# The second MLP product of six token chunks in seven block products for eight, with the sums on GpSimd and all of it in 128x64 tiles

## The chip, the cores and the metric

The kernel runs on one core of a Trainium2 chip. The metric is the device time of one execution in microseconds (us); lower is better. Five engines matter: PE (TensorE, the matrix unit, with its weight loads shown as PEld), DVE (VectorE), ACT (ScalarE), POOL (GpSimd), and SP, whose queue issues most of the DMAs.

## The reference, cut to what matters

The input of the MLP is the output of a linear attention with 4 batches, 4 heads, 1088 tokens and head width 32. The tokens are the rows of a 4352 x 128 matrix. The MLP goes to 2048 hidden channels and back to 128.

```python
def phi(x):                       # 64 features of a token: all products of two 8-wide sketches
    a = np.einsum('rd,bhsd->bhsr', S1, x)
    b = np.einsum('rd,bhsd->bhsr', S2, x)
    return np.einsum('bhsi,bhsj->bhsij', a, b).reshape(*x.shape[:-1], r * r)
q_p, k_p = (phi(q), phi(k))
kv = np.einsum('bhsf,bhsd->bhfd', k_p, v)
z = np.sum(k_p, axis=2)
x = (q_p @ kv) / (q_p @ z + 1e-06)          # per batch and head
...
x = np.ascontiguousarray(attn_out.transpose(0, 2, 1, 3)).reshape(B * S, H * D)   # 4352 x 128
h = x @ w_in                                 # 4352 x 2048
g = 0.5 * h * (1.0 + erf(h * inv_sqrt2))
return (g @ w_out).astype(np.float32)        # 4352 x 128
```

The change is about the last line, `g @ w_out`.

## The kernel before, in words

**Chunks and steps.** The tokens are cut into nine chunks: chunks 0 to 7 have 512 tokens each (two a batch, `NMAIN = 8`), chunk 8 has the 64 last tokens of each batch, 256 in all. The 2048 hidden channels are cut into 16 tiles of 128 (`NF`). One step is one chunk `n` and one tile `fi`. The list `steps` has 144 of them: chunks 0 and 1 alternate in groups of four, and from step 32 on it is chunk after chunk, 16 steps each.

**What a step does.** `hidden(n, fi)` multiplies a 128x128 tile of `w_in` with the turned attention output `xT[n]` (128 channels x 512 tokens) into a PSUM bank (`h_ps`, two buffers, line 488), and ACT takes it through Gelu into a tile `g` (line 490). `project`, two steps later (`LAG = 2`), multiplies a 128x128 tile of `w_out` with that `g` and adds it up over the 16 tiles in one PSUM bank (`o_ps`, two buffers, line 503). All values are fp32, and a product of fp32 values is two matmul instructions. When the 16 tiles are done, `store` turns the bank with one DVE transpose (line 513) and issues the DMAs to the output.

**The attention of later chunks** is put into steps of earlier ones by the calls `at(t, f, ...)`: `slots[t]` holds what is issued in step `t`. For chunk `n` that is `query_turn` (a DVE transpose), `query_expand` (four matmuls at line 393, four ACT copies at line 400 into the tile `A_sb`, four DVE multiplications at line 414) and `attend` (matmuls at line 434, four ACT copies into `den` at line 440, a DVE reciprocal at line 441, four DVE multiplications at line 445 that write `xT[n]`). For batch `b` it is `widen_v` and `widen_v_rem` on POOL (lines 287 and 295, with memsets), `key_turn_blocks` (four DVE transposes, line 304), `features` (matmuls at line 319, copies on ACT, multiplications on DVE at line 333), `finish_keys` (matmuls at lines 353 and 360) and `turn_kv` (a transpose on PE, line 369). They use the four PSUM banks of `w_ps`.

**The weights** come in as 64-bit numbers and are rounded to fp32 in the kernel by `Rounding`, piece by piece (`CUTS`), during chunks 0 and 1.

**Order.** Each engine takes its instructions in the order of the text; a loop at the end of the function adds dependencies that keep it. Within a step the order is `hidden`, then `store` of a finished chunk, then `slots[t]`, then `project_at(t)`:

```python
    def project_at(t):
        if LAG <= t < len(steps) + LAG:
            project(*steps[t - LAG])
            if steps[t - LAG][1] == NF - 1:
                done.append(steps[t - LAG][0])
```

Of the kernel before, what the change touches and what calls it, by code (L numbers as in the profile page):

```python
# [8 lines left out]
FP = mybir.dt.float32  # L9
U32 = mybir.dt.uint32  # L10
# [6 lines left out]
def kernel(  # L17
# [18 lines left out]
    pe, dve, act, pool, sp = nc.tensor, nc.vector, nc.scalar, nc.gpsimd, nc.sync  # L36
# [3 lines left out]
    d_model = out.shape[1]  # L40
    d_ff = moe_w_in.shape[1]
    NF = d_ff // 128
# [5 lines left out]
    CW = JC * 128  # L48
    G = 128 // 32
    NCH = J // JC  # L50
    C = D + 1
    LAG = 2
    NMAIN = B * NCH
    NCHUNK = NMAIN + 1
    assert B == 4 and d_model == 128 == H * D == JC * D == 2 * F and H == 4 and REM == 64 and NCH == 2

    big = ctx.enter_context(tc.tile_pool(name="big", bufs=1))
    att = ctx.enter_context(tc.tile_pool(name="att", bufs=2))
    mlp = ctx.enter_context(tc.tile_pool(name="mlp", bufs=2))
# [8 lines left out]
    def work_bank():  # L68
        return work_banks()[:, 0]
# [7 lines left out]
    def out_bank():  # L77
        return ops.tile([128, CW], FP, name="o_ps")
# [4 lines left out]
    LC = 512  # L83
    pieces = list(zip(CUTS, CUTS[1:]))
# [30 lines left out]
    def load_rem(n, b):  # L115
        sp.dma_start(out=rem[n][b // 2 * REM:(b // 2 + 1) * REM, b % 2],
                     in_=src_of[n][b, :, MAIN:S, :].rearrange("h p d -> p h d"))

    def landing(dst, wide):

        if wide:
            raw[dst.name] = big.tile([dst.shape[0], dst.shape[1], 2], U32, name=f"raw_{dst.name}")
            return raw[dst.name].rearrange("p n two -> p (n two)")
        return dst

# [247 lines left out]
    qT, qp, xT = {}, {}, {}  # L373
# [104 lines left out]
    g_of, o_of = {}, {}  # L478

    def w_tile(w, fi):  # L480
        i = max(i for i, (c0, c1) in enumerate(pieces) if c0 <= fi * 128)
        at = fi * 128 - CUTS[i]
        return w[i][:, at:at + 128]

    def hidden(n, fi):
        W = width[n]
        ps = hidden_bank()
        pe.matmul(ps[:, :W], lhsT=w_tile(w_in_sb, fi), rhs=xT[n][:, :W], start=True, stop=True)  # L488
        g_of[n, fi] = mlp.tile([128, CW], FP, name="g", bufs=4)
        act.activation(out=g_of[n, fi][:, :W], in_=ps[:, :W], func=ACT.Gelu)  # L490

    def project(n, fi):
        first, final = fi == 0, fi == NF - 1
        if first:
            o_of[n] = out_bank()
        g = g_of.pop((n, fi))
        if n == NMAIN:

            for i in range(B // 2):
                pe.matmul(o_of[n][:, i * 128:(i + 1) * 128], lhsT=g[:, i * 128:(i + 1) * 128], rhs=w_tile(w_out_sb, fi),  # L500
                          start=(first and i == 0), stop=final, skip_group_check=True)
            return
        pe.matmul(o_of[n], lhsT=w_tile(w_out_sb, fi), rhs=g, start=first, stop=final)  # L503
    def store(n):
        oT = mlp.tile([128, JC, d_model], FP, name="oT")
        if n == NMAIN:
            for i, (copy, eng) in enumerate(((by_dve, sp), (by_act, act))):
                copy(out=oT[:, i, :], in_=o_of[n][:, i * 128:(i + 1) * 128])  # L508
                for b in (i, i + 2):
                    eng.dma_start(out=out[b * S + MAIN:(b + 1) * S, :], in_=oT[b // 2 * REM:(b // 2 + 1) * REM, i, :])  # L510
            return

        dve.transpose(out=oT.rearrange("p n d -> p (n d)"), in_=o_of[n])  # L513
        row = n // NCH * S + n % NCH * CW
        if n < NCH:
# [17 lines left out]
    bank = work_bank()  # L533
    keep_busy(3, bank)
    r = Rounding(SR)
# [72 lines left out]
    def at(t, f, *a):  # L608
        slots[t].append(lambda: f(*a))
# [29 lines left out]
    for i, (t0, t1) in enumerate(((4, 6), (8, 10), (12, 20))):  # L639
        round_at(t0, w_in_sb[i + 2])  # L640
        round_at(t1, w_out_sb[i + 2])
    for b in range(1, B):
        t = NCH * b * NF
        for r in range(2):
            at(t - 20, widen_v, b, r)
        at(t - 20, widen_v_rem, b)
        for r in range(2):
            at(t - 18, key_turn_blocks, b, r)
        for r in range(2):
            at(t - 17, features, b, r)  # L650
        if b == 1:
            at(t - 16, turn_keys_rem, b)
            at(t - 15, features_rem, b)
        at(t - 14, finish_keys, b)
        at(t - 13, lambda b=b: turn_kv(b, held["kv"], by_dve))
    for n in range(2, NCHUNK):
        t = n * NF
        at(t - 13, query_turn, n)
        at(t - 12, query_expand, n)
        at(t - 8, attend, n)  # L660

    def project_at(t):
        if LAG <= t < len(steps) + LAG:
            project(*steps[t - LAG])
            if steps[t - LAG][1] == NF - 1:
                done.append(steps[t - LAG][0])

    done = []
    for t in range(len(steps) + LAG):
        if t == 3:  # L670

            attend_by_token(1, halves(work_banks()), lambda: (w_out[1].mantissas(), w_out[1].signs(),
                                                              w_out[1].product(pool)))
        if t == 4:
            turn_x(1, work_bank())
            project_at(t)
        if t < len(steps):
            hidden(*steps[t])
        while done:
            store(done.pop())  # L680
        for f in slots[t]:
            f()
        if t != 4:
            project_at(t)
    while done:
        store(done.pop())


    last = {}
# [36 lines left out]
```

## Time and profile before

| what | before |
|---|---|
| median of 3 runs | 289.57 us (288.95 to 289.64) |
| the profiled execution, its own time | 289.47 us |
| its span in the profile | 287.3 us |
| granted TensorE clock | 0.998 |
| busy PE, DVE, ACT, POOL | 280.7, 121.8, 134.4, 15.6 us |
| matmul instructions of `hidden` (line 488) | 288 |
| matmul instructions of `project` (line 503 / chunk 8, line 500) | 256 / 64 |

The span is the time from the first to the last instruction in the profile; the 2.2 us between it and the execution's time lie around it. A row of a group gives line, engine and operation, output and inputs, shapes and count, then busy time, the mean of one in ns, and the idle time of the engine just before these instructions with what ended it. A row of the timeline gives start, duration, engine, line, and how many instructions are merged in it. Matmuls overlap in the pipeline, so what counts for PE is the distance from start to start and not the duration of one.

### The profile page before, as it was taken

The numbers are of one execution on the slowest core, as the hardware profiler recorded it, in microseconds if no ns is written. First come the engines' busy times: TensorE is split into PE (matmuls) and PEld (weight loads), VectorE is DVE, ScalarE is ACT, GpSimd is POOL, SyncE is SP. The second block draws the span as 40 slices with busy tenths as digits, with TensorE's granted clock in tenths as the row PEclk, the third lists the DMA queues.
The fourth block names the chain that finished last, engine by engine and source line by source line (L and its number), as shares of the span: only waits on it lengthen the run. The fifth ranks groups of instructions, "written<-read, shape, count | busy, mean of one in ns | idle before, by whom it ended". The sixth has DMA issues, their size and how long they took to land.

```text
span 287.3 us, 3822 instructions
## 1 busy us (share of the span) xinstructions
PE 280.7 (98%) x1479; PEld 135.8 (47%) x1479; DVE 121.8 (42%) x196; ACT 134.4 (47%) x258; POOL 15.6 (5%) x44
## 2 busy tenths in 40 slices
PE   8989999999999999999999999999999999999994
PEld 6744444643444344543444344544444344444793
DVE  5996888163713093233513184234313351231000
ACT  4683774266335633255335533256335633453341
POOL 3331040300000000300000000000000000000000
PEclk9999999999999999999999999999999999999999
DMA  7568532535012000200001000200010000100010
GB/s 210 174 196 277 140 82 65 167 73 147 2 30 34 9 0 2 37 2 0 0 12 27 0 2 0 39 0 0 0 28 10 0 0 9 27 2 0 16 20 18
DMA packets 37904, 13.36 MB, mean 46 GB/s; under 512 B 28288, under 2 KB 37248, under 8 KB 37888
## 3 DMA queue, kind: packets, MB, share of 16 engines
q1 hardware_dynamic: 37648, 13.05, 18.2%
q8 instruction: 11, 0.18, 0.3%
q10 hardware_dynamic: 240, 0.08, 0.1%
q14 instruction: 5, 0.04, 0.0%
HBM read 10.90 MB, written 2.23 MB: 46 GB/s over the span
## 4 chain that ended last, share of the span: by engine, by line
PE 96%; DVE 1%; ACT 0%; issue 0%
PE h_ps L488 41%; PE o_ps L503 39%; PE w_ps L393 3%; PE o_ps L500 2%; PE w_ps L434 2%; PE w_ps L353 2%; PE w_ps L531 1%; PE w_ps L319 1%; PE o_ps L353 1%; PE h_ps L274 1%; PE h_ps L459 0%; PE w_ps L459 0%; PE o_ps L274 0%; DVE xT L473 0%; DVE bits_a L224 0%
## 5 line engine op out<-in xcount | busy, mean ns | idle before, releaser
L490 ACT ACTIVATE g<-h_ps 128x512 f32<-128x512 f32 (+1 forms) x144 | 82.5, 573 | 127.7 <-PE h_ps L488 127.4
L488 PE MATMUL h_ps<-xT,w_in 128*128 128x512 f32 (+1 forms) x288 | 140.2, 570 | 1.1 <-DVE xT L473 1.0
L503 PE MATMUL o_ps<-g,w_out 128*128 128x512 f32 x256 | 132.9, 601 | 0.0
L488 PEld LDWEIGHTS h_ps<-xT,w_in 128*128 128x128 f32 x288 | 53.4, 190 | 63.8 <-issue 60.0
L503 PEld LDWEIGHTS o_ps<-g,w_out 128*128 128x128 f32 x256 | 46.5, 190 | 59.0 <-issue 57.7
L441 DVE RECIPROCAL den<-den 128x512 f32<-128x512 f32 (+1 forms) x7 | 21.9, 3124 | 44.0 <-ACT den L440 44.0
L414 DVE TENSOR_TENSOR q_pT<-A_sb,w_ps 64x512 f32<-64x512 f32 x32 | 22.1, 691 | 24.0 <-ACT A_sb L400 23.3
L513 DVE STREAM_TRANSPOSE oT<-o_ps 128x512 f32<-128x512 f32 x8 | 5.7, 717 | 43.9 <-PE o_ps L503 43.9
L400 ACT COPY A_sb<-w_ps 64x512 f32<-64x512 f32 (+1 forms) x36 | 17.7, 557 | 3.1 <-PE w_ps L393 3.0
L445 DVE TENSOR_TENSOR xT<-w_ps,den 32x512 f32<-32x512 f32 (+1 forms) x28 | 18.2, 649 | 1.0
L440 ACT ACTIVATE den<-w_ps 32x512 f32<-32x512 f32 (+1 forms) x28 | 15.6, 557 | 3.0 <-PE w_ps L434 2.7
L333 DVE TENSOR_TENSOR k_p<-a_t,w_ps 128x512 f32<-128x512 f32 x12 | 8.0, 686 | 7.9 <-ACT a_t L332 7.9
L287 POOL COPY v_aug<-v 128x512 f32<-128x512 f32 x8 | 5.5, 699 | 86.3 <-PE w_ps L353 73.2
L500 PEld LDWEIGHTS o_ps<-w_out,g 128*128 128x128 f32 x64 | 9.3, 191 | 0.7
L500 PE MATMUL o_ps<-w_out,g 128*128 128x128 f32 x64 | 9.4, 274 | 0.0
L393 PE MATMUL w_ps<-qT,Srep 32*128 32x512 f32 x64 | 9.1, 640 | 0.0
L230 ACT ACTIVATE bits_r<-bits_e,below 128x512 uint32<-128x512 uint32 (+2 forms) x11 | 6.7, 611 | 1.5 <-DVE bits_e L222 1.4
L434 PE MATMUL w_ps<-q_pT,kz 64*64 64x512 f32 (+1 forms) x80 | 7.2, 458 | 0.0
L353 PEld LDWEIGHTS w_ps<-k_p,v_aug 128*64 128x64 f32 x192 | 5.8, 138 | 2.3 <-issue 2.3
L238 DVE SCALAR_TENSOR_TENSOR bits_m<-bits_a,bits_low 128x512 f32<-128x512 uint32 (+2 forms) x10 | 5.8, 584 | 2.4 <-ACT bits_low L218 1.7
L353 PE MATMUL w_ps<-k_p,v_aug 128*64 128x64 f32 x192 | 6.3, 224 | 0.0
L508 DVE COPY oT<-o_ps 128x128 f32<-128x128 f32 x1 | 0.3, 291 | 12.5 <-PE o_ps L500 12.5
(119 smaller groups left out, 114.6 us busy)
## 6 DMA issues: line engine op xcount, KB each, us to landing
raw_w_in<-in_moe_w_in_dram SPq DMA_DIRECT2D x3, 512.0 KB, 6.6
raw_w_out<-in_moe_w_out_dram SPq DMA_DIRECT2D x3, 512.0 KB, 9.5
k<-in_k_dram SPq DMA_DIRECT2D x48, 32.0 KB, 1.8
v<-in_v_dram SPq DMA_DIRECT2D x3, 512.0 KB, 4.3
q<-in_q_dram SPq DMA_DIRECT2D x24, 64.0 KB, 3.7
out_dram<-oT SPq DMA_DIRECT2D x24, 64.0 KB, 2.2
k<-in_k_dram SPq DMA_DIRECT2D x2, 256.0 KB, 2.9
q<-in_q_dram SPq DMA_DIRECT2D x2, 256.0 KB, 3.8
```

Source lines behind the costliest of these rows:

```text
L353: pe.matmul(ps[c * 64:(c + 1) * 64, r * F:(r + 1) * F], lhsT=v_aug[:, 2 * c + r, i, :], rhs=k_p[b, r][:, t, c * 4 + ch * 2 + one].rearrang ...
L393: pe.matmul(B_of[n][g // 2][:, g % 2, :W], lhsT=Srep[rows].rearrange("p a i j -> p (a i j)"), rhs=qT[n][rows].rearrange("p h j t -> p (h j ...
L400: act.copy(out=A[g // 2][F:, g % 2, :width[n]], in_=B_of[n][g // 2][:F, g % 2, :width[n]])
L414: dve.tensor_mul(out=cols[r * F:(r + 1) * F], in0=a[:, :, r::2], in1=b[:, :, r::2])
L434: pe.matmul(banks[r][c * F:(c + 1) * F, c0:c1], lhsT=kz[b][r * F:(r + 1) * F, c, :], rhs=qp[n][r * F:(r + 1) * F, c, c0:c1], start=True, s ...
L440: act.activation(out=den[h * D:(h + 1) * D, :W], in_=banks[r][at:at + D, :W], func=ACT.Copy, bias=1e-6)
L441: dve.reciprocal(out=den[:, :W], in_=den[:, :W])
L445: dve.tensor_mul(out=xT[n][rows, :W], in0=banks[h % 2][rows, :W], in1=den[rows, :W])
L488: pe.matmul(ps[:, :W], lhsT=w_tile(w_in_sb, fi), rhs=xT[n][:, :W], start=True, stop=True)
L490: act.activation(out=g_of[n, fi][:, :W], in_=ps[:, :W], func=ACT.Gelu)
L500: pe.matmul(o_of[n][:, i * 128:(i + 1) * 128], lhsT=g[:, i * 128:(i + 1) * 128], rhs=w_tile(w_out_sb, fi), start=(first and i == 0), stop= ...
L503: pe.matmul(o_of[n], lhsT=w_tile(w_out_sb, fi), rhs=g, start=first, stop=final)
```

## The change

**The product by blocks.** For chunks 2 to 7 the second product is computed in blocks: the 512 tokens in two halves of 256, the 128 output channels in two halves of 64, and the tiles `fi` in pairs. For one pair, that is a 2x2 by 2x2 product of blocks, eight block products of 128x64 weights by 256 tokens in the plain form. The new form makes seven of them from sums of blocks, numbered 1 to 7 (6 is added in two places, `6a` and `6b`). `channel_sums` makes the sums of weight blocks (`T[1]` to `T[4]`), once for each piece of `w_out`. `token_sums` makes four sums of blocks of `g`, for four steps (`NB = 4`, two pairs) at a time. Both are on POOL.

**Tiles.** Two block products are issued together, one into partitions 0 to 63 and one into 64 to 127 of PSUM, so each uses one half of the array's columns (`PLACE` has half, bank and column). A chunk adds up in both `o_ps` banks. `hidden` of these chunks, and of the first five tiles of chunk 8, is issued as two products of 64 columns each instead of one of 128.

**Putting the parts together.** `combine(n)` copies both banks to SBUF (one by DVE, one by ACT), moves parts between the halves of the partitions with two more ACT copies, and makes six additions on DVE. `store` turns its result.

**Order.** The block products of four steps are issued as 3, 2 and 2 pairs, 3 to 5 steps after the last of the four (first block of a chunk), or as 2, 2, 1 and 2 pairs, 2 to 5 steps after it (other blocks). `store` and `combine` of a chunk come in step 5 of the next chunk, ahead of `slots[t]`. The keys of batches 2 and 3 and the turning and expanding of queries from chunk 3 on come two steps earlier; `attend` stays. The products of chunk 8's first tiles are put later, behind the last block products of chunk 7.

**Buffers.** The landing buffers of the raw weights become tiles of two rings (`block`, three buffers, and `small`, four), which later hold `g` and the weight sums. The token sums take over the tiles of `Rounding`, and `combine` those of `A_sb`. The DMAs and their order stay as they were.

```diff
--- before.py
+++ after.py
@@ -51,6 +51,8 @@
     C = D + 1
     LAG = 2
     NMAIN = B * NCH
+    FAST = 2
+    NB = 4
     NCHUNK = NMAIN + 1
...
+    def block(dtype=U32):
...
+        b = big.tile([128, NB, 512], U32, name="block", bufs=3)
...
+    def small(dtype):
...
+        t = big.tile([128, 512], U32, name="small", bufs=4)
...
-    def hidden(n, fi):
+    def hidden(n, fi, by_halves=False):
         W = width[n]
         ps = hidden_bank()
-        pe.matmul(ps[:, :W], lhsT=w_tile(w_in_sb, fi), rhs=xT[n][:, :W], start=True, stop=True)
-        g_of[n, fi] = mlp.tile([128, CW], FP, name="g", bufs=4)
+        w = w_tile(w_in_sb, fi)
+        for rows in (slice(0, 64), slice(64, 128)) if by_halves else (slice(0, 128),):
+            pe.matmul(ps[rows, :W], lhsT=w[:, rows], rhs=xT[n][:, :W], start=True, stop=True)
+        if n < FAST:
+            g_of[n, fi] = mlp.tile([128, CW], FP, name="g", bufs=4)
+        else:
+            if fi % NB == 0:
+                blocks[n, fi // NB] = block(FP)
+            g_of[n, fi] = blocks[n, fi // NB][:, fi % NB]
         act.activation(out=g_of[n, fi][:, :W], in_=ps[:, :W], func=ACT.Gelu)
+    blocks, sums, acc = {}, {}, {}
+    T = {}
+    HW = CW // 2
+    NPAIR = NF // 2
+    PLACE = {"1": (0, 0, 0), "2": (0, 0, HW), "3": (1, 0, 0), "7": (1, 0, HW),
+             "4": (0, 1, 0), "6a": (0, 1, HW), "6b": (1, 1, 0), "5": (1, 1, HW)}
+    def channel_sums(i):
+        if not T:
+            for j in range(1, 5):
+                T[j] = small(FP).rearrange("p (n d) -> p n d", d=64)
+        c0, c1 = pieces[i]
+        at = slice(c0 // 256, c1 // 256)
+        w = w_out_sb[i].rearrange("p (n two d) -> p n two d", two=2, d=d_model)
+        b11, b12, b21, b22 = (w[:, :, k, c * 64:(c + 1) * 64] for k in range(2) for c in range(2))
+        t1, t2, t3, t4 = (T[j][:, at] for j in range(1, 5))
+        pool.tensor_sub(out=t1, in0=b12, in1=b11)
+        pool.tensor_sub(out=t3, in0=b22, in1=b12)
+        pool.tensor_sub(out=t2, in0=b22, in1=t1)
+        pool.tensor_sub(out=t4, in0=b21, in1=t2)
+    def token_sums(n, b):
+        g = blocks[n, b].rearrange("p (e two) (half x) -> p e two half x", two=2, half=2)
+        a11, a21, a12, a22 = (g[:, :, k, h] for k in range(2) for h in range(2))
+        s = {}
+        for j, (name, dtype) in enumerate((("bits_a", U32), ("bits_e", U32), ("bits_low", FP), ("bits_m", FP))):
+            t = mlp.tile([128, LC], dtype, name=name)
+            s[j + 1] = (t if dtype == FP else t.bitcast(FP)).rearrange("p (e x) -> p e x", e=2)
+        pool.tensor_add(out=s[1], in0=a21, in1=a22)
+        pool.tensor_sub(out=s[3], in0=a11, in1=a21)
+        pool.tensor_sub(out=s[2], in0=s[1], in1=a11)
+        pool.tensor_sub(out=s[4], in0=a12, in1=s[2])
+        sums[n, b] = s
+    def factor(n, b, name, e):
+        k = 2 * b + e
+        if name in "12":
+            fi = 2 * k + int(name) - 1
+            return g_of[n, fi][:, 0:HW], w_tile(w_out_sb, fi)[:, 0:64]
+        if name == "3":
+            return sums[n, b][4][:, e], w_tile(w_out_sb, 2 * k + 1)[:, 64:128]
+        if name == "4":
+            return g_of[n, 2 * k + 1][:, HW:], T[4][:, k]
+        j = {"5": 1, "6": 2, "7": 3}[name[0]]
+        return sums[n, b][j][:, e], T[j][:, k]
+    def two_products(n, b, i):
+        two = [("4", "5", 0, 0), ("4", "5", 1, 1), ("1", "7", 0, 0), ("1", "7", 1, 1), ("6a", "6b", 0, 1),
+               ("2", "3", 0, 0), ("2", "3", 1, 1)][i]
+        if b == 0 and i == 0:
+            acc[n] = [out_bank(), out_bank()]
+        for name, e in zip(two[:2], two[2:]):
+            half, bank, col = PLACE[name]
+            moving, fixed = factor(n, b, name, e)
+            pe.matmul(acc[n][bank][half * 64:(half + 1) * 64, col:col + HW], lhsT=fixed, rhs=moving,
+                      start=b == 0 and i in (0, 2), stop=b == NF // NB - 1, skip_group_check=True)
+    def combine(n):
+        N = att.tile([128, 2, CW], FP, name="A_sb", bufs=2)
+        C = att.tile([128, 2, CW], FP, name="A_sb", bufs=2)
+        dve.tensor_copy(out=N[:, 0], in_=acc[n][0])
+        act.copy(out=N[:, 1], in_=acc[n][1])
+        flat = N.rearrange("p a b -> p (a b)")
+        lo, hi = slice(0, 64), slice(64, 128)
+        act.copy(out=C[lo, 0], in_=flat[hi, HW:3 * HW])
+        dve.tensor_add(out=C[lo, 1], in0=N[lo, 1], in1=C[lo, 0])
+        dve.tensor_add(out=C[lo, 0, 0:HW], in0=N[lo, 0, 0:HW], in1=C[lo, 1, HW:])
+        act.copy(out=C[hi, 0, 0:HW], in_=C[lo, 0, 0:HW])
+        dve.tensor_add(out=C[lo, 1, HW:], in0=C[lo, 1, 0:HW], in1=C[lo, 0, 0:HW])
+        dve.tensor_add(out=C[lo, 1, 0:HW], in0=N[lo, 0, 0:HW], in1=N[lo, 0, HW:])
+        dve.tensor_add(out=C[hi, 0, HW:], in0=C[hi, 0, 0:HW], in1=N[hi, 1, HW:])
+        dve.tensor_add(out=C[hi, 1].rearrange("p (two x) -> p two x", two=2),
+                       in0=N[hi, 0].rearrange("p (two x) -> p two x", two=2),
+                       in1=C[hi, 0, None, HW:].broadcast_to([64, 2, HW]))
+        return C[:, 1]
...
-        dve.transpose(out=oT.rearrange("p n d -> p (n d)"), in_=o_of[n])
+        dve.transpose(out=oT.rearrange("p n d -> p (n d)"), in_=o_of[n] if n < FAST else combine(n))
...
+    for i in range(len(pieces)):
+        at(22 + i, channel_sums, i)
     for b in range(1, B):
-        t = NCH * b * NF
+        t = NCH * b * NF - (0 if b == 1 else 2)
         for r in range(2):
             at(t - 20, widen_v, b, r)
         at(t - 20, widen_v_rem, b)
...
         at(t - 13, lambda b=b: turn_kv(b, held["kv"], by_dve))
     for n in range(2, NCHUNK):
         t = n * NF
-        at(t - 13, query_turn, n)
-        at(t - 12, query_expand, n)
+        early = 0 if n == 2 else 2
+        at(t - 13 - early, query_turn, n)
+        at(t - 12 - early, query_expand, n)
         at(t - 8, attend, n)
-    def project_at(t):
-        if LAG <= t < len(steps) + LAG:
-            project(*steps[t - LAG])
-            if steps[t - LAG][1] == NF - 1:
-                done.append(steps[t - LAG][0])
-
-    done = []
+    products = {t: [] for t in range(len(steps) + LAG)}
+    done = {t: [] for t in range(len(steps) + LAG + 1)}
+    for t, (n, fi) in enumerate(steps):
+        if n < FAST:
+            products[t + LAG].append((project, n, fi))
+            if fi == NF - 1:
+                done[t + LAG + 1].append(n)
+        elif n == NMAIN:
+            at_ = max(t + LAG, (n * NF + 5) if fi < 3 else (n * NF + 6) if fi < 5 else 0)
+            products[at_].append((project, n, fi))
+            if fi == NF - 1:
+                done[at_ + 1].append(n)
+        elif fi % NB == NB - 1:
+            b = fi // NB
+            for later, pairs in (((3, 3), (4, 2), (5, 2)) if b == 0 else ((2, 2), (3, 2), (4, 1), (5, 2))):
+                for i in range(pairs):
+                    products[t + later].append((two_products, n, b, len([p for q in products.values() for p in q
+                                                                        if p[:3] == (two_products, n, b)])))
+            if b == NF // NB - 1:
+                done[t + 6].append(n)
...
             turn_x(1, work_bank())
-            project_at(t)
+            for f, *a in products[t]:
+                f(*a)
         if t < len(steps):
-            hidden(*steps[t])
-        while done:
-            store(done.pop())
+            n, fi = steps[t]
+            hidden(n, fi, by_halves=n >= FAST and (n < NMAIN or fi < 5))
+        for n in done[t]:
+            store(n)
+        if t < len(steps) and FAST <= steps[t][0] < NMAIN and steps[t][1] % NB == NB - 1:
+            token_sums(steps[t][0], steps[t][1] // NB)
         for f in slots[t]:
             f()
         if t != 4:
-            project_at(t)
-    while done:
-        store(done.pop())
+            for f, *a in products[t]:
+                f(*a)
+    for n in done[len(steps) + LAG]:
+        store(n)
```

`NPAIR` is not used. In the changed kernel `project` serves chunks 0, 1 and 8.

More of the change, by code (lines that the diff above doesn't have):

```diff
@@ L117, in load_rem @@
                      in_=src_of[n][b, :, MAIN:S, :].rearrange("h p d -> p h d"))
+    half_block = []
+    def block(dtype=U32):
+        b = big.tile([128, NB, 512], U32, name="block", bufs=3)
+        return b if dtype == U32 else b.bitcast(dtype)
+    def small(dtype):
+        t = big.tile([128, 512], U32, name="small", bufs=4)
+        return t if dtype == U32 else t.bitcast(dtype)
     def landing(dst, wide):
         if wide:
-            raw[dst.name] = big.tile([dst.shape[0], dst.shape[1], 2], U32, name=f"raw_{dst.name}")
+            rows, n = dst.shape
+            if n == 512:
+                if not half_block:
+                    half_block.append(block())
+                    r = half_block[0][:, 0:2]
+                else:
+                    r = half_block.pop()[:, 2:4]
+                raw[dst.name] = r.rearrange("p a b -> p (a b)").rearrange("p (n two) -> p n two", two=2)
+            elif n == 256:
+                raw[dst.name] = small(U32).rearrange("p (n two) -> p n two", two=2)
+            else:
+                raw[dst.name] = big.tile([rows, n, 2], U32, name=f"raw_{dst.name}")
             return raw[dst.name].rearrange("p n two -> p (n two)")
@@ L483, in w_tile @@
         return w[i][:, at:at + 128]
-    def hidden(n, fi):
+    def hidden(n, fi, by_halves=False):
         W = width[n]
         ps = hidden_bank()
-        pe.matmul(ps[:, :W], lhsT=w_tile(w_in_sb, fi), rhs=xT[n][:, :W], start=True, stop=True)
-        g_of[n, fi] = mlp.tile([128, CW], FP, name="g", bufs=4)
-        act.activation(out=g_of[n, fi][:, :W], in_=ps[:, :W], func=ACT.Gelu)
+        w = w_tile(w_in_sb, fi)
[3 more added lines that the diff above has]
+            g_of[n, fi] = mlp.tile([128, CW], FP, name="g", bufs=4)
+        else:
+            if fi % NB == 0:
+                blocks[n, fi // NB] = block(FP)
+            g_of[n, fi] = blocks[n, fi // NB][:, fi % NB]
+        act.activation(out=g_of[n, fi][:, :W], in_=ps[:, :W], func=ACT.Gelu)
@@ L494, in project @@
         if first:
-            o_of[n] = out_bank()
+            o_of[n] = out_bank() if n < NMAIN else work_bank()
         g = g_of.pop((n, fi))
```

## The prediction

> **What bounds the kernel now.** I read first the page's busy times and the chain that ended last:
>
> ```profile
> PE 280.7 (98%) x1479; PEld 135.8 (47%) x1479; DVE 121.8 (42%) x196; ACT 134.4 (47%) x258; POOL 15.6 (5%) x44
> PE 96%; DVE 1%; ACT 0%; issue 0%
> L490 ACT ACTIVATE g<-h_ps 128x512 f32<-128x512 f32 (+1 forms) x144 | 82.5, 573 | 127.7 <-PE h_ps L488 127.4
> L488 PE MATMUL h_ps<-xT,w_in 128*128 128x512 f32 (+1 forms) x288 | 140.2, 570 | 1.1 <-DVE xT L473 1.0
> L503 PE MATMUL o_ps<-g,w_out 128*128 128x512 f32 x256 | 132.9, 601 | 0.0
> ```
>
> TensorE is the bound from end to end; its waits in the groups of both products come to 1.1 us, and ScalarE waits for it. Every fp32 product is two matmul instructions (288 for 144). Then the PE timeline of chunk 2, around one `attend`:
>
> ```profile
> 95.71 1.02 PE L488 MATMUL h_ps<-xT,w_in 128*128 128x512 f32 x2
> 96.66 1.09 PE L434 MATMUL w_ps<-q_pT,kz 64*64 64x512 f32 x8
> 97.68 1.13 PE L503 MATMUL o_ps<-g,w_out 128*128 128x512 f32 x2
> 98.64 1.02 PE L488 MATMUL h_ps<-xT,w_in 128*128 128x512 f32 x2
> 99.50 1.02 PE L503 MATMUL o_ps<-g,w_out 128*128 128x512 f32 x2
> ...
> 180.03 2.09 PE L353 MATMUL w_ps<-k_p,v_aug 128*64 128x64 f32 x64
> ```
>
> The start of L488 to that of L503 is 0.86 us without interruption, so an instruction of 512 columns takes 0.429 us and a step (hidden plus project) 1.717. Eight 64x64 instructions on four tiles hold the array 1.02 us, two rounds of 0.429 and 0.16 more: tiles overlap. The 64 instructions of 128x64, on two column halves, take (2.09 - 0.22)/32 = 0.058 us a pair, where 64/512 of 0.429 is 0.054.
>
> **What the Trainium skill says.** "TensorEngine Tiling (Array Packing)", Key Properties: tiles work independently, a change of mode drains the array. Both agree with the lines above. "SBUF — State Buffer", Who interferes with whom: a DVE instruction with two SBUF inputs and a GpSimd instruction that reads SBUF exclude each other for a whole instruction. The timeline shows it:
>
> ```profile
> 37.58 0.69 DVE L248 TENSOR_TENSOR w_in<-bits_m,bits_e 128x512 f32<-128x512 f32 x1
> 37.62 1.88 POOL L287 COPY v_aug<-v 128x512 f32<-128x512 f32 x2 [13.06 <-DMA v<-in_v_dram]
> 38.19 0.83 DVE L222 TENSOR_SCALAR bits_e<-raw_w_out 128x512 uint32<-128x512 uint32 x1
> ```
>
> Two POOL copies that take 0.61 each alone (at 117.59 us) took 1.88 together, and L222, 0.43 on average on raw_w_in, took 0.83. "GPSIMD Engine Reference", Elementwise: a two-input add of 2048 fp32 takes 4497 ns. The trace has a 128x256 one at 0.728 us and copies of 64 and 512 columns at 0.24 and 0.61, thus about 0.18 fixed; 512 elements of two inputs are 0.18 + 2 x 0.55 = 1.27 us by the trace.
>
> **The change, part by part.** I count in steps of a chunk, 0 to 15, and call S8 the start of `hidden` in step 8. The order of PE's instructions is the text's.
>
> *Gain.* For four steps before: 16 instructions x 0.429 = 6.866 us. After: `hidden` by halves, 8 pair slots of 512 columns, and seven pairs of block products, 14 slots of 256. The price of a slot lies between pure scaling (0.429 and 0.2145) and 0.005 more (L353); I take 0.430 and 0.216[...]: 8 x 0.430 + 14 x 0.216 = 6.464. Saved 0.402 a block, x 24 blocks = **9.6 us** (7.7 to 10.3). Weight loads double in number but are half as wide, and L353 hides two in 0.058 us. Excursions to other modes keep their number but for L353 (now in mode) and the transpose L369 (now out), twice each: zero, 0.5 either way.
>
> *Sums on GpSimd.* Four ops a block, 4 x 1.27 = 5.1 us in 6.5: fits. The first is wanted some 4.1 us after the block's last `hidden` starts, the last 8.9 after; they are ready at 1.7 + 1.3 = 3.0 and 6.9. Hidden. `widen_v` with its memsets (2.7 us, chunks 2 and 4) stands ahead of a block's sums and takes 1.4 of that slack; cost zero. `channel_sums` runs at steps 22 to 26 of the whole, ahead of its first use at 38: zero. SP's queue and the DMAs stay.
>
> *Combine, five times within chunks 3 to 7.* It is issued in step 5, after `hidden`. T is the end of the last product, also S5. PE has without the next gelu: `hidden` 5 and 6, three pairs, `hidden` 7, two pairs: 3 x 0.86 + 5 x 0.433 = 4.75. Then `hidden` 8 wants the bank that gelu 6 frees, and gelu 6 is queued on ACT behind combine's copies. gelu 5 starts at T + 1.05 (as 1.06 behind `hidden` at L490), copy of `acc` 1.55 to 2.15, copy across partitions to 2.8, then ACT's third copy waits for two DVE adds (0.69 and 0.42, both inputs in SBUF), then gelu 6. With the port free: adds done at 4.0, gelu 6 done at 5.0: PE loses 0.3. But GpSimd is on block 0's sums: `hidden` 3 starts at T - 3.05, its gelu waits for the expand's copies until T - 1.95, the sums run back to back from T - 1.27 to T + 3.85. The first add asks at 2.85, in the fourth sum, and gets the port at 3.85. gelu 6 ends at 6.05: PE loses **1.3**, five times 6.5 us (0.3 to 2.0 each). The PSUM banks themselves come free in time: DVE's at T + 0.95, ACT's at 2.2, wanted at 1.73 and 2.6. After chunk 7 the sums are done and PE has 3.9 us of other work: 0.3.
>
> *Keys two steps earlier (batches 2 and 3).* `features` goes from step 15 to 13. Its matmuls wait for `key_turn_blocks` on DVE, which stands behind `attend`'s reciprocal:
>
> ```profile
> 100.23 3.35 DVE L441 RECIPROCAL den<-den 128x512 f32<-128x512 f32 x1 [6.61 <-ACT den L440]
> 103.69 2.79 DVE L445 TENSOR_TENSOR xT<-w_ps,den 32x512 f32<-32x512 f32 x4
> 106.51 1.42 DVE L304 STREAM_TRANSPOSE kT<-k 128x256 f32<-128x256 f32 x4
> ```
>
> With S8 = 95.71 the first half of kT is there at S8 + 11.6 and all at 12.2. Before, PE came for it at 109.89, S8 + 14.2. Now: step 8 2.95 (with attend), 9 and 10 1.73, 11 1.3, 12 1.73, and `hidden` 13: S8 + 10.3. PE loses 1.3 + 0.1, **2.8 us** for both (0 to 4). The queue order behind (`finish_keys`, query transpose, expand) keeps its distances.
>
> *Start of the scheme.* Steps 34 to 37 have only `hidden` on PE (0.86) while ACT has four gelus and the expand's four copies (89.70 to 91.72, 2.0 us). `hidden` 37 needs gelu 35, done near S34 + 4.8; PE would be there at 3.7: **1.2 us** (0.8 to 1.6). The work left out there is done later, so it is no gain.
>
> Sum: -9.6 + 6.5 + 0.3 + 2.8 + 1.2 = +1.2 us on the profiled execution's 289.47 (span 287.3), thus 290.7. That execution stands 0.1 under the median 289.57.
>
> **The rivals.** *Port free (faster).* If the first add of combine doesn't have to wait for a whole sum (sums shorter, as the 1.07 us of the one 128x512 two-input op on POOL, whose inputs are broadcast, or shifted), combine costs 0.3 to 0.7 a chunk: -9.6 + 2.5 + 0.3 + 2.0 + 1.2 = -3.6: 285.9. For it: the reserve of 4.75 us nearly covers the chain. Against it: GpSimd is busy 80% of the time. It decides at (9.6 - 2.8 - 1.2 - 0.3)/5 = 1.06 us lost a combine: below, the kernel is faster. *GpSimd the bound (slower).* Over 1.6 us a sum, by port waits, a block takes 4 ops instead of 6.46: at 1.8, 7.3 us, 24 x 0.43 over before = +10 and the rest: about 301. Against it: 0.728 for 256 elements even beside DVE work. *The halves don't overlap fully.* It would not do what it says: 0.012 us more a slot is 22 x 24 x 0.012 = 6.3 us: 297. Against it: 0.058 a pair in L353; were they serial, it would be 0.107.
>
> **How the numbers follow.** Stalls eat the gain: 0.55, 287.5 to 294. Port free: 0.33, 283.5 to 288. GpSimd bound: 0.06. Poor overlap: 0.06. A measurement of this kernel tells about 0.3%, 0.87 us, from no change. Faster: 0.33 and an eighth of the first case, 0.40; within: 0.12; slower: 0.36 of the first case and both last ones, 0.48. The range from 283.5 to 297.5 leaves out the GpSimd-bound case and the tails, under 2 in 10.
>
> **What would show it.** Per step: four steps without excursion in 6.4 to 6.5 us (over 6.6, the overlap is poor); PE waits in `hidden` for ACT once a chunk, in step 8, of 1.3 us, and ACT's third copy in combine waiting for DVE, whose first add is recorded with over 1 us instead of 0.69 (at 0.69, the lock argument is wrong); PE waits at `features` for DVE 1.4 us in chunks 2 and 4; POOL's sums near 1.27 us and no PE wait for Pool. A PE wait for Pool in every block, or a time under 284 or over 298, would make the account wrong.

## The result, and the profile after

| | before | after |
|---|---|---|
| median | 289.61 us, 4 runs (288.95 to 289.79) | 291.43 us, 4 runs (291.22 to 291.66) |
| ratio, 95% interval | 1 | 1.0067 (1.005 to 1.0085) |
| profiled execution, span | 289.47 us, 287.3 us | 291.22 us, 289.4 us |
| granted clock | 0.998 | 0.997 |

The change costs 1.8 us, 0.5% to 0.85% of the time; 290.7 was predicted. The page of the kernel after, with its busy times, its chain by engine, the groups of the two products and one of the four groups of token sums:

```profile
PE 273.4 (94%) x2161; PEld 138.2 (48%) x2161; DVE 149.6 (52%) x238; ACT 142.7 (49%) x276; POOL 146.0 (50%) x160
PE 79%; DVE 9%; ACT 8%; issue 3%; DVEq 0%; ACTq 0%
L516 PE MATMUL h_ps<-xT,w_in 128*64 128x512 f32 (+3 forms) x490 | 140.7, 577 | 8.2 <-ACT block L523 7.0
L561 POOL TENSOR_TENSOR bits_m<-block,bits_e 128x512 f32<-128x512 f32 x24 | 30.6, 1275 | 1.9
L587 PE MATMUL o_ps<-block,w_out 128*64 128x256 f32 x192 | 50.9, 382 | 0.0
```

TensorE's busy time fell by 7.3 us while the span grew by 2.1. The chain now passes through DVE and ACT for 17% of the span, where it was 1%. The group of `hidden` waits 8.2 us where it waited 1.1. GpSimd takes 1.27 us a sum, and no wait stands before the block products (line 587). The waits of PE in the kernel after, with their releaser, total, number and longest:

```profile
PE h_ps L516 <- ACT block L523: 7.0, 6, 1.3
PE w_ps L345 <- DVE kT L330: 1.9, 2, 0.9
```

The first line is `hidden` waiting for a Gelu: once in each of chunks 3 to 7 and once at the start of the scheme. The second is `features` waiting for the turned keys, in chunks 2 and 4. The timeline of the kernel after shows the first wait, from step 5 of chunk 3, where `combine` of chunk 2 is issued:

```profile
122.77 1.89 PE L516 MATMUL h_ps<-xT,w_in 128*64 128x512 f32 x8
...
123.84 0.60 ACT L523 ACTIVATE block<-h_ps 128x512 f32<-128x512 f32 x1 [1.04 <-PE h_ps L516]
124.33 0.58 ACT L595 COPY A_sb<-o_ps 128x512 f32<-128x512 f32 x1
124.95 0.62 ACT L599 COPY A_sb<-A_sb 64x512 f32<-64x512 f32 x1
125.49 1.27 POOL L561 TENSOR_TENSOR bits_m<-block,bits_e 128x512 f32<-128x512 f32 x1
125.60 1.70 DVE L600 TENSOR_TENSOR A_sb<-A_sb 64x512 f32<-64x512 f32 x1 [1.92 <-ACT A_sb L599]
127.33 0.42 DVE L601 TENSOR_TENSOR A_sb<-A_sb 64x256 f32<-64x256 f32 x1
127.84 0.40 ACT L602 COPY A_sb<-A_sb 64x256 f32<-64x256 f32 x1 [2.27 <-DVE A_sb L601]
128.26 1.08 ACT L523 ACTIVATE block<-h_ps 128x512 f32<-128x512 f32 x2
128.92 1.08 PE L516 MATMUL h_ps<-xT,w_in 128*64 128x512 f32 x4 [1.25 <-ACT block L523]
```

The reader is to see a chain over four engines. DVE's add at 125.60 takes 1.70 us and ends 0.54 after GpSimd's fourth sum (125.49 + 1.27 = 126.76). ACT's copy L602 has waited 2.27 us for the two adds, and the Gelu of step 6 stands behind that copy. `hidden` of step 8 needs the bank that this Gelu frees.

**Account by steps.** The distance from one `hidden` to the next gives each step its length. An undisturbed step of the kernel after is step 9 of chunk 2:

```profile
97.16 1.03 PE L516 MATMUL h_ps<-xT,w_in 128*64 128x512 f32 x4
98.02 0.38 PE L587 MATMUL o_ps<-block,small 128*64 128x256 f32 x1
...
98.24 0.38 PE L587 MATMUL o_ps<-block,small 128*64 128x256 f32 x1
...
98.88 1.03 PE L516 MATMUL h_ps<-xT,w_in 128*64 128x512 f32 x4
```

`hidden` takes 0.86 us, and a slot of the block products 0.22; there are four such slots in this step. Over four steps, with seven pairs, that is 1.72 + 1.72 + 1.29 + 1.72 = 6.455 us, against 6.866 before, so a block of four saves 0.411.

| term | predicted | measured |
|---|---|---|
| gain, 24 blocks | -9.6 | -9.9 |
| combine in chunks 3 to 7 (step 7: 3.14 or 3.15 for 1.72, the last 2.99) | 6.5 | 7.0 |
| keys early (step 13 of chunks 2 and 4: 4.23 and 4.20 for 2.94, which such a step takes in e1 below) | 2.8 | 2.55 |
| start, steps 34 to 37 | 1.2 | 1.1 |
| steps 32 and 33 (2.06 each for 1.72) | none | 0.7 |
| chunk 8 and the last combine | 0.3 | 1.1 |
| sum | 1.2 | 2.55 |

What PE does for the attention within chunks 2 to 7 became 0.5 us cheaper, all that lies before chunk 2 was 0.24 shorter, and the last step, with the output, 0.3 longer (6.40 for 6.10). That leaves the 2.1 between the two spans.

### The profile page after: what moved, and what is told of

It is laid out like the page before. It is cut to its first block, busy times and chain, and to the rows that moved or that the text cites. A ratio compares the mean times of both kernels' runs of the same rounds, so it can differ in the third digit from the quotient of the medians.

```text
span 289.4 us, 5444 instructions
## 1 busy us (share of the span) xinstructions
PE 273.4 (94%) x2161; PEld 138.2 (48%) x2161; DVE 149.6 (52%) x238; ACT 142.7 (49%) x276; POOL 146.0 (50%) x160
## 4 chain that ended last, share of the span: by engine, by line
PE 79%; DVE 9%; ACT 8%; issue 3%; DVEq 0%; ACTq 0%
PE h_ps L516 35%; PE o_ps L587 19%; PE o_ps L622 10%; DVE A_sb L600 3%; PE w_ps L419 3%; PE w_ps L460 2%; DVE den L467 2%; PE w_ps L379 2%; ACT den L466 2%; PE w_ps L619 2%; ACT block L523 1%; PE w_ps L345 1%; ACT A_sb L599 1%; DVE xT L471 1%; ACT A_sb L595 1%
## 5 line engine op out<-in xcount | busy, mean ns | idle before, releaser
L516 PE MATMUL h_ps<-xT,w_in 128*64 128x512 f32 (+3 forms) x490 | 140.7, 577 | 8.2 <-ACT block L523 7.0
L523 ACT ACTIVATE block<-h_ps 128x512 f32<-128x512 f32 (+1 forms) x112 | 62.8, 567 | 82.7 <-PE h_ps L516 81.7
L558 POOL TENSOR_TENSOR bits_a<-block 128x512 f32<-128x512 f32 x24 | 31.9, 1329 | 76.1 <-ACT block L523 76.0
L516 PEld LDWEIGHTS h_ps<-xT,w_in 128*64 128x64 f32 (+1 forms) x490 | 43.8, 146 | 46.0 <-issue 18.0
L587 PE MATMUL o_ps<-block,w_out 128*64 128x256 f32 x192 | 50.9, 382 | 0.0
L622 PE MATMUL o_ps<-g,w_out 128*128 128x512 f32 x64 | 33.4, 603 | 0.0
L561 POOL TENSOR_TENSOR bits_m<-block,bits_e 128x512 f32<-128x512 f32 x24 | 30.6, 1275 | 1.9
L560 POOL TENSOR_TENSOR bits_e<-bits_a,block 128x512 f32<-128x512 f32 x24 | 30.6, 1275 | 0.0
L559 POOL TENSOR_TENSOR bits_low<-block 128x512 f32<-128x512 f32 x24 | 30.5, 1273 | 0.0
L622 PEld LDWEIGHTS o_ps<-g,w_out 128*128 128x128 f32 x64 | 11.3, 190 | 14.3 <-issue 13.5
```

The source lines that it names most:

```text
L516: pe.matmul(ps[rows, :W], lhsT=w[:, rows], rhs=xT[n][:, :W], start=True, stop=True)
L558: pool.tensor_add(out=s[1], in0=a21, in1=a22)
L559: pool.tensor_sub(out=s[3], in0=a11, in1=a21)
L560: pool.tensor_sub(out=s[2], in0=s[1], in1=a11)
L561: pool.tensor_sub(out=s[4], in0=a12, in1=s[2])
L587: pe.matmul(acc[n][bank][half * 64:(half + 1) * 64, col:col + HW], lhsT=fixed, rhs=moving, start=b == 0 and i in (0, 2), stop=b == NF // N ...
```

## The experiments

The theory: TensorE gains what was worked out, and single waits use it up. The largest is `combine`, since DVE's adds cannot have SBUF while GpSimd is in a sum. Rivals: the copies on ACT cost by themselves, whatever GpSimd does; and the 64-column tiles cost time of their own. The median of before beside the runs was 289.45 us for the first four, 289.54 for the next four and 289.73 for the last three. Lengths of steps are read as above. Changes against "after" set each median against 291.43.

**e1_features_later.**

```diff
-            at(t - 17, features, b, r)
+            at(t - (17 if b == 1 else 16), features, b, r)
```

> The changed kernel with the keys' features of batches 2 and 3 in step 14 instead of 13; all else stays. Theory (PE waits at features for the transposed keys, 1.4 us in chunks 2 and 4): both waits go, 291.4 - 2.8 = 288.6 us. Rival (the wait only moves on: finish_keys, which stays in step 16, then finds the features late): 290.5 to 291.5 us, with a PE wait at the key sum.

Measured: 289.21 us, ratio 0.999 (0.9983 to 0.9998), 2.2 below after. The waits of PE in this kernel:

```profile
PE h_ps L516 <- ACT block L523: 7.0, 6, 1.3
PE w_ps L651 <- DVE idle L228: 1.2, 1, 1.2
```

The wait for the keys is gone, and the 7.0 us for ACT stay. Step 13 is 1.72 in both chunks. Step 14, which now has `features`, takes 2.94: 1.72 and 1.22 for the matmuls of `features`. Steps 13 and 14 together are 1.29 and 1.26 shorter, 2.55 in all. The loss through the keys is independent of the others.

**e2_fourth_sum_dve.** The fourth token sum of the first block of chunks 3 to 7 goes from GpSimd to DVE, behind the adds that `combine` needs first.

```diff
-        pool.tensor_sub(out=s[4], in0=a12, in1=s[2])
+        if b == 0 and n > FAST:
+            late_sum[n] = dict(out=s[4], in0=a12, in1=s[2])
+        else:
+            pool.tensor_sub(out=s[4], in0=a12, in1=s[2])
...
         act.copy(out=C[hi, 0, 0:HW], in_=C[lo, 0, 0:HW])
+        if n + 1 in late_sum:
+            dve.tensor_sub(**late_sum.pop(n + 1))
```

> The changed kernel with the fourth token sum of a chunk's first block (chunks 3 to 7) made by DVE inside combine, behind its second add, instead of by GpSimd. Theory (combine's first add waits for the port that the fourth sum holds): the add is recorded with 0.69 instead of 1.70 us, PE's wait in step 8 falls from 1.42 to about 0.3 us, five times: 291.4 - 5.6 = 285.8 us. Rival (the chain of copies and adds is long by itself, the port does not matter): within 0.5 us of 291.4.

Measured: 286.44 us, ratio 0.9899 (0.9881 to 0.9917), 5.0 below after. The waits of PE and the adds of the same `combine` on DVE's timeline:

```profile
PE h_ps L516 <- ACT block L523: 2.0, 6, 0.9
```

```profile
125.91 0.68 DVE L603 TENSOR_TENSOR A_sb<-A_sb 64x512 f32<-64x512 f32 x1 [1.92 <-ACT A_sb L602]
126.63 0.42 DVE L604 TENSOR_TENSOR A_sb<-A_sb 64x256 f32<-64x256 f32 x1
126.97 0.68 DVE L607 TENSOR_TENSOR bits_m<-block,bits_e 128x512 f32<-128x512 f32 x1
```

The same first add takes 0.68 us instead of 1.70: GpSimd's third sum ended at 125.73, before it. Step 7 is 2.12 in all five chunks, which leaves 0.40 of the 1.42: that much of the rival is true, the chain over ACT costs it without GpSimd. One sum moved in each of five chunks brings the kernel 1.0% below the one before. The last add of `combine` (line 611) now meets the next block's first sum and takes 1.65 instead of 0.69, but nothing waits for it. The sum itself is cheaper on DVE (0.68) than on GpSimd (1.27).

**e3_third_copy_dve.** Another way to the same end: the copy that held up the Gelu goes from ACT to DVE.

```diff
-        act.copy(out=C[hi, 0, 0:HW], in_=C[lo, 0, 0:HW])
+        dve.tensor_copy(out=C[hi, 0, 0:HW], in_=C[lo, 0, 0:HW])
```

> The changed kernel with combine's third copy made by DVE instead of ACT, so that ACT waits for no add. Theory (PE waits since gelu 6 is queued on ACT behind that copy): no wait in step 8, five times 1.4 and 0.4 at the end: 291.4 - 7.4 = 284.0 us, although the first add still waits for the port. Rival (PE waits for the PSUM banks, or for DVE): 289 us or more.

Measured: 288.40 us, ratio 0.9977 (0.9956 to 0.9999): 3.0 below after, not the 7.4 expected. Step 7 is back to 1.72 in all five chunks, so the wait in `hidden` is gone as expected. But chunk 4 became longer, step 13 from 4.20 to 8.47 and step 14 from 1.72 to 2.54, together 5.1. PE's waits, then DVE's timeline in chunk 4, in this kernel:

```profile
PE w_ps L345 <- DVE kT L330: 4.8, 2, 3.8
PE h_ps L516 <- ACT block L523: 0.9, 1, 0.9
```

```profile
155.76 1.24 DVE L602 COPY A_sb<-A_sb 64x256 f32<-64x256 f32 x1
157.01 1.40 DVE L603 TENSOR_TENSOR A_sb<-A_sb 64x256 f32<-64x256 f32 x1
158.44 1.39 DVE L604 TENSOR_TENSOR A_sb<-A_sb 64x256 f32<-64x256 f32 x1
159.84 1.41 DVE L605 TENSOR_TENSOR A_sb<-A_sb 64x256 f32<-64x256 f32 x1
...
162.94 3.31 DVE L467 RECIPROCAL den<-den 128x512 f32<-128x512 f32 x1
...
169.16 1.42 DVE L330 STREAM_TRANSPOSE kT<-k 128x256 f32<-128x256 f32 x4
```

In the kernel after, these three adds took 0.42 us each; here each takes 1.40, as long as a sum. Beside them GpSimd's timeline of this kernel has the next block's sums:

```profile
155.49 1.36 POOL L558 TENSOR_TENSOR bits_a<-block 128x512 f32<-128x512 f32 x1 [0.76 <-ACT block L523]
156.81 1.31 POOL L559 TENSOR_TENSOR bits_low<-block 128x512 f32<-128x512 f32 x1
```

The Gelus come earlier now, so GpSimd starts block 1 sooner, inside `combine` (1.9 us sooner, counted from the start of the chunk). DVE and GpSimd then alternate, and each small add waits for a whole sum. That happens in all five chunks; in chunk 4 it costs time, since there the keys stand behind it: the reciprocal of `attend` queues behind the adds, the keys behind the reciprocal, and PE waits for the keys. PE waits 2.9 us longer than in the kernel after (3.8 for 0.9). The other 2.2 of the 5.1 are slower matmuls. From 169.6 to 174.0 us the granted TensorE clock was 0.50, and PE's slots are 0.43 apart instead of 0.22:

```profile
171.50:174.00 2.50, 2.50 (x14) 1.24 (x12) 1.94 (x4) 0.54 (x3) 0.00 (x0) 0.50 0.00 0
172.00 0.63 PE L587 MATMUL o_ps<-block,small 128*64 128x256 f32 x1
172.43 0.63 PE L587 MATMUL o_ps<-block,small 128*64 128x256 f32 x1
```

(The first line is a stretch with its length, the busy times of PE, PEld, DVE, ACT and POOL with their instructions, the granted clock 0.50, and the DMAs.) In the same stretch of work in the kernel after, the clock is 1.00. So five waits of 1.4 us went, and 5.1 us came back in one place. This is why the gain fell short of the 7.4 expected.

**e4_no_token_sums.** The block products read blocks of `g` in place of their sums.

```diff
-            token_sums(steps[t][0], steps[t][1] // NB)
+            plain_sums(steps[t][0], steps[t][1] // NB)
...
+        sums[n, b] = {1: a21, 2: a22, 3: a11, 4: a12}
```

> The changed kernel without the token sums: the block products read the blocks of g in place of their sums, so the values differ from the reference; the matmuls, their shapes and their order stay. Theory (GpSimd costs time only through the port in combine and through its lateness in chunk 8): 291.4 - 5.5 - 0.6 = 285.3 us, the rate of undisturbed steps unchanged at 6.46 us for four. Rival (GpSimd's sums also pace the steps): under 284 us and quicker steps.

Measured: 286.12 us (one run), 5.3 below after. PE waits 2.0 us for ACT as in e2, step 7 is 2.12 again, and four undisturbed steps are 6.455 us as with the sums. So 96 sums cost TensorE nothing but the lock inside `combine` and one thing more: in chunk 8 step 4 is 1.39 here and 1.87 after. There the steps are short (256 tokens), and the last pairs of chunk 7 come before the last sum is done. First the kernel after, then this one:

```profile
270.08 1.28 POOL L561 TENSOR_TENSOR bits_m<-block,bits_e 128x512 f32<-128x512 f32 x1
271.42 0.43 PE L587 MATMUL o_ps<-bits_m,w_out 128*64 128x256 f32 x1
...
266.23 1.03 PE L593 MATMUL o_ps<-block,w_out 128*64 128x256 f32 x8
```

The product with `bits_m` starts at 271.42, just after the sum ends at 271.36; without the sum the two pairs follow `hidden` in one piece.

**e5_tiles_alone.** The kernel before, with both products of chunks 2 to 7 in two 64-column tiles and no sums.

```diff
-        pe.matmul(ps[:, :W], lhsT=w_tile(w_in_sb, fi), rhs=xT[n][:, :W], start=True, stop=True)
+        w = w_tile(w_in_sb, fi)
+        for rows in (slice(0, 64), slice(64, 128)) if 2 <= n < NMAIN else (slice(0, 128),):
+            pe.matmul(ps[rows, :W], lhsT=w[:, rows], rhs=xT[n][:, :W], start=True, stop=True)
```

(and the same for `project`.)

> The kernel before, with both products of chunks 2 to 7 issued as two products of 64 columns each; plain sums, no block scheme. Theory (a pair of halves costs what the whole costs): within 0.7 us of the kernel before, 289.6 to 290.3. Rival (0.005 us a slot more, as the short pairs of the key sum have it): 96 steps x 4 slots x 0.005 = 1.9 us more, 291.5.

Measured: 290.64 us, ratio 1.0035 (1.0022 to 1.0047). PE's timeline of this kernel, first where whole and halved products alternate, then where all are halved:

```profile
81.03 1.08 PE L490 MATMUL h_ps<-xT,w_in 128*64 128x512 f32 x4
82.04 1.13 PE L507 MATMUL o_ps<-g,w_out 128*128 128x512 f32 x2
83.10 1.08 PE L490 MATMUL h_ps<-xT,w_in 128*64 128x512 f32 x4
...
86.07 1.03 PE L507 MATMUL o_ps<-g,w_out 128*64 128x512 f32 x4
86.93 1.03 PE L490 MATMUL h_ps<-xT,w_in 128*64 128x512 f32 x4
87.79 1.03 PE L507 MATMUL o_ps<-g,w_out 128*64 128x512 f32 x4
```

The time is 0.3 above the theory's range and 0.9 below the rival's number; the steps tell why. All in halves: 0.86 us a product and 1.717 a step, the same as with whole products before. Where forms alternate, 82.04 to 83.10 and 81.03 to 82.04 make 2.07 a step: 0.35 for two changes of form. Two such steps at the head of chunk 2 and two in chunk 8 (1.64 for 1.29) are 1.4 us of loss, against 1.3 between the spans (288.6 and 287.3). The kernel after has the same two steps at its start (80.47 to 82.54 and on, 2.06 each). A single change, from the whole products of chunk 1 to the halves, shows as 0.09 (step 15 of chunk 1 with 1.81 for 1.72, here and in the kernel after).

**e6_hidden_whole.** The other side of it: `hidden` whole, block products in halves, so the form changes in nearly every step.

```diff
-            hidden(n, fi, by_halves=n >= FAST and (n < NMAIN or fi < 5))
+            hidden(n, fi, by_halves=False)
```

> The changed kernel with hidden in one product of 128 columns throughout, the block products in 64 columns as before. Theory (each change of tile form costs about 0.17 us, as steps 32 and 33 of the changed kernel show with 2.07 instead of 1.72 us): 88 to 94 steps x 0.35 = 31 to 33 us more, about 323 us. Rival (the change of form is hidden behind the stream and those two steps were long for another reason): 291 us.

Measured: 309.66 us (one run), less than the 323 expected. An undisturbed step is 2.07, as expected. The sum is smaller, because the waits vanish under it: step 7 is 2.07 rather than 3.14 and the step with `features` 3.13 rather than 4.2; and most steps in which PE also works for the attention grow by only 0.05 to 0.2. So `hidden` has to be halved for the block products to gain anything.

**e7_start.** `hidden` of the first two steps of chunk 2 whole, and the expanding of chunk 3's queries, which fell into the starting steps, three steps earlier.

```diff
-        early = 0 if n == 2 else 2
+        early = {2: 0, 3: 5}.get(n, 2)
...
-            hidden(n, fi, by_halves=n >= FAST and (n < NMAIN or fi < 5))
+            hidden(n, fi, by_halves=n >= FAST and (n < NMAIN or fi < 5) and (n, fi) not in ((2, 0), (2, 1)))
```

> The changed kernel with hidden of the first two steps of chunk 2 in one product of 128 columns, and query_turn and query_expand of chunk 3 three steps earlier (steps 30 and 31), while PE still has plain products. Theory: 0.7 us of tile form changes and 1.0 us of waiting for ACT go: 289.7 us. Rival (the work is only moved in front of the same stretch): 291.0 us or more.

Measured: 289.84 us, ratio 1.0009 (0.9999 to 1.002), 1.6 below after. Steps 32 and 33 are 1.72 and 1.81, and PE's wait after step 36 is gone. The two terms at the start are confirmed together (1.8 in the account), not each by itself.

**e8_all.** The edits of e1, e3 and e7 in one kernel.

> The changed kernel with the features later, the third copy on DVE and the two edits at the start together. Theory (the losses are separate and add up): 291.4 - 2.8 - 7.4 - 1.7 = 279.5 us, 3.5% under the kernel before. Rival (a wait taken away gives way to the next one): 282 to 285 us.

Measured: 283.18 us, ratio 0.9788 (0.9773 to 0.9804). The rival was right: the delay of the keys seen in e3 is smaller with `features` a step later, but not gone. Step 14 of chunk 4 is 5.37 where e1 has 2.94. PE's waits in this kernel:

```profile
PE w_ps L345 <- DVE kT L330: 2.3, 2, 2.1
```

In this trace, the fastest of the five runs, the clock stays at 1.00 behind that wait. The four others took 283.11 to 284.17 at a mean clock of 0.993 for 0.998; whether they lost clock there, as e3 did, no trace shows.

**e9_rest_later.** e8, with the last four adds of `combine` and the output transpose in step 15, behind `features`; after chunk 7 at once.

```diff
...
+    for n in range(FAST, NMAIN - 1):
+        at((n + 1) * NF + 15, store, n, True)
```

> The kernel of e8_all with combine cut in two: its copies and the first two adds stay in step 5, its last four adds and the output transpose go to step 15 of the same chunk, behind the keys' features (after chunk 7 they stay together). Theory (in e8_all DVE comes late to the reciprocal in chunk 4, since each late add waits for a whole sum on GpSimd, and PE waits 2.4 us for the transposed keys): that wait goes, 283.2 - 2.4 = 280.8 us. Rival (the lateness is handed on to the key sum or the next query): 282.5 us or more.

Measured: 284.57 us, ratio 0.983 (0.9789 to 0.9871). No gain, as the rival had it. Chunk 4's wait is gone (step 14 is 2.94), but chunk 5's step 1 takes 6.17 instead of 2.13. PE's waits and DVE's timeline in this kernel:

```profile
PE w_ps L395 <- DVE kv_T L392: 3.0, 1, 3.0
```

```profile
169.37 1.50 DVE L609 TENSOR_TENSOR A_sb<-A_sb 64x256 f32<-64x256 f32 x1
170.91 1.38 DVE L610 TENSOR_TENSOR A_sb<-A_sb 64x256 f32<-64x256 f32 x1
...
176.04 0.25 DVE L392 COPY kv_T<-w_ps 128x128 f32<-128x128 f32 x1
```

The adds met GpSimd's sums in the new place too, at 1.4 to 1.5 us each, and `turn_kv`'s copy was the one that queued behind them. After this wait of 3.0 us the clock was again 0.50 (from 176 to 178 us). In e3, e8 and e9 moving DVE's adds only chose who comes late.

**e10_fourth_sum_all.** So the sum is taken out of the way of the first adds, and the copy stays on ACT: the edits of e1, e2 and e7.

> The changed kernel with the features later, both edits at the start, and the fourth sum on DVE (third copy on ACT as in the changed kernel). Theory (the gains of the single runs add up): 286.4 - 2.2 - 1.6 = 282.6 us, no wait for keys in chunk 4, 0.4 us in step 8. Rival (DVE late in chunk 4 as in e3_third_copy_dve): 285 us or more.

Measured: **282.32 us, ratio 0.9732 (0.9699 to 0.9765)**, the fastest of all, and the only one whose whole interval lies more than 2% below the kernel before. The first add of DVE's `combine` in chunk 4 and the reciprocal behind it, then PE's waits:

```profile
151.95 0.68 DVE L603 TENSOR_TENSOR A_sb<-A_sb 64x512 f32<-64x512 f32 x1 [1.92 <-ACT A_sb L602]
...
158.84 3.35 DVE L467 RECIPROCAL den<-den 128x512 f32<-128x512 f32 x1 [1.48 <-ACT den L466]
```

```profile
PE h_ps L516 <- ACT block L523: 1.1, 5, 0.2
```

The reciprocal waits for its own input, no longer for `combine`, and the wait for keys is absent. The gains add up: 5.0, 2.2 and 1.6 alone make 8.8, and the kernel is 9.1 below after. What is left of the account is the 9.9 gained, less 2.0 in five `combine`s (0.40 each) and 1.1 in chunk 8: 6.8 us, against 6.7 between the spans (287.3 and 280.6).

**e11_six_sums.** The test from the other side, with more sums: the fourth sum three times, six GpSimd instructions a block.

```diff
-        pool.tensor_sub(out=s[4], in0=a12, in1=s[2])
+        for _ in range(3):
+            pool.tensor_sub(out=s[4], in0=a12, in1=s[2])
```

> The changed kernel with the fourth token sum made three times over (six instructions a block on GpSimd, the same values). Theory (GpSimd has a reserve of about a fifth; 6 x 1.27 = 7.6 us a block is over the 6.46 of four undisturbed steps, a chunk is 30.5 us of sums and up to 3 more beside them against 28.7 to 32.2 now): GpSimd sets the pace, PE waits for sums in most blocks, 298 to 304 us. Rival (the excursions of PE give room enough): under 294 us.

Measured: 310.13 us (one run), above the range expected. PE's waits in this kernel:

```profile
PE o_ps L588 <- POOL bits_m L562: 10.0, 10, 2.5
PE h_ps L516 <- ACT block L523: 10.0, 6, 2.3
```

PE now waits for a sum ten times (in the kernel after only once, in chunk 8), and the wait through `combine` grew as well. Four sums a block fit beside PE's work, six do not. The excess over the kernel after is spread over chunks 2 to 8, most of it in chunk 8 (4.6 us), and is not split further.

## Why the prediction came out right, and where it didn't

- **The gain** was right: -9.9 measured for -9.6. A slot of the block products costs 0.2156 us and one of `hidden` 0.4296, a little under the 0.216 and 0.430 taken.
- **Combine** was right in its chain, and with 7.0 for 6.5 nearly in size. Counted from S5 = 122.77, the Gelu of step 6 was to end at 6.05 and ended at 6.09; the fourth sum was to end at 3.85 and ended at 3.99. The lost 1.42 lies above the 1.06 from which the outcome turns. That GpSimd's sum is the cause is shown by e2 (first add 0.68, step 7 shorter by 1.02) and by e4; with it the rival that has the port free falls. The Trainium skill, "SBUF — State Buffer", Who interferes with whom, says that a DVE instruction with two SBUF inputs contends with a GpSimd instruction that reads SBUF; the prediction took the lock from there, and the add's 1.70 against 0.68 agrees. Of the prediction's own example, the row L222 has one SBUF input and is not the case that it quotes; e3's copy, with one input too, was held all the same.
- **Keys** were right, 2.55 for 2.8, and e1 shows them to be separate. **GpSimd's sums** at 1.27 us are as estimated, and PE waits for none before chunk 8; without them the undisturbed steps are as long (e4). So the rival with GpSimd as the bound falls.
- **Halves that overlap poorly** falls with e5: 1.72 a step.
- **Start** was right for steps 34 to 37 (1.1 for 1.2). Missed were steps 32 and 33, in which halved `hidden` alternates with whole `project`. The Trainium skill, "TensorEngine Tiling (Array Packing)", Key Properties, was cited for the drain at a change of mode, and the prediction counted only excursions to other modes. Where the forms alternate, the runs price a change at 0.35/2 = 0.17 us (e5, e6); 0.7 was left out.
- **The end** cost 1.1 for 0.3. The 0.3 for the last `combine` held: steps 7 and 8 of chunk 8 lost 0.4. Not foreseen was step 4, which lost 0.57, of which 0.47 is the last sum (e4) and 0.1 a change of form, and step 5 with 0.1 for another. The step that failed is "Hidden": it took all sums to be ready in time, from the length of steps with 512 tokens, and the steps of chunk 8 have 256. Nine pairs of block products there are moved work and no loss.
- **Costs taken as nothing** held: `turn_kv`'s step is 2.13 for 1.83, against a step with the key sum that is 0.34 shorter, and beside `widen_v` PE waits for no sum.

The account ends 1.35 above the prediction's sum: 1.5 from the two misses and 0.5 from `combine`, less 0.65 from the gain, the keys and the start. The attention and what lies before chunk 2 gave some back, so the span grew by 2.1 for the 1.2 forecast. What lies around the span fell from 2.2 to 1.8 us, which nobody forecast, and the median ended 0.7 above. The path and the waits were foreseen; that the number came so close is partly luck, since errors of both signs met.

## What to carry to other kernels

When work moves to GpSimd, look at which DVE instructions with two SBUF inputs run at the same time, and follow who is queued behind them: here the cost appeared on a third engine. A wait removed by moving one instruction can return at the next consumer of the same queue (e3, e9), so take away the collision on the path that matters (e2, e10). A long wait of TensorE can cost more than its length: look at the granted clock behind it (e3, e9). Keep products of one tile form together: in this kernel 128x64 tiles in pairs are free, and the changes between them and 128x128 are not.

## What the runs showed of the hardware that I had not expected

- Where 128x128 and 128x64 products alternate, each change costs 0.17 us (two in a step, 2.06 to 2.07 us for 1.72, in after, e5 and e6; e7 lacks those steps and their cost), while the halved form itself costs nothing (0.86 us a product in both).
- DVE's small adds against back-to-back GpSimd sums wait for a whole sum every time, not once: 1.40, 1.39 and 1.41 us instead of 0.42 (e3), and 1.50, 1.38 and 1.40 (e9). DVE's copy of 64x256, which has one input, met the same (1.24; 0.29 after chunk 7, where GpSimd is idle). Not held were DVE's products with one input in PSUM and the reciprocal: 0.70 and 3.35 us beside running sums (lines 471 and 467, after), as in the kernel before.
- During PE's waits of 3.8 us (e3) and 3.0 us (e9) the granted clock fell to 0.50 and stayed there for 2 us and more of the work that followed. After the wait of 2.1 us in the trace of e8 it was 1.00. What decides it, these runs do not show.
